# Routed experts: tokens put in expert order by one-hot matmuls and block scatters instead of row scatters

## The chip, the cores and the metric

One core of a Trainium2 chip runs the whole program: its five engines are TensorE (PE), VectorE (DVE), ScalarE (ACT), GpSimd (POOL) and SyncE (SP), beside the DMA queues. The metric is device time in microseconds, the median over runs; less is better.

## The reference

Three stages follow each other on 22784 tokens (4 x 5696) of 128 numbers. First a causal long convolution by FFT, then a soft mixture of experts with 32 slots, then a top-1 mixture of 8 experts. Only the last stage is touched:

```
logits = x @ w_gate + modality_bias[modality_id]
e_idx = argmax(logits, axis=1)
probs = exp(logits - max); probs /= probs.sum + 1e-09
gate_w = probs[arange(N), e_idx]
for e in range(8):
    mask = e_idx == e
    h = maximum(x[mask] @ w1[e], 0)
    out[mask] = gate_w[mask] * (h @ w2[e])
```

The input of this stage is itself a weighted sum of 32 slot outputs, so a token is carried as its 32 weights `c`, and the slot outputs are folded into the first weights of the expert. With the inputs used, all tokens choose one expert, so there are exactly 89 full tiles of 256 tokens and the program's part for a larger number of tiles doesn't run.

## The kernel before

The routing (class `Routing`) works on 178 groups of 128 tokens: token p*178+g sits on partition p in group g. DVE chooses the expert, counts tokens by expert with scans, and gets each token's position in expert order (`choose`, `gates`, `offsets`, `positions`). A record of 34 numbers a token (32 weights, gate, token id: 136 bytes) is written by POOL to `s_rec` in memory with an indirect DMA, one of 128 rows for each group (L1071).

The table GB cuts the groups into 9 chunks, CP the chunks into 3 parts. A tile of 256 records may be loaded when every group that can hold its tokens has been scattered; `first` and `chunk_of` say which. The part for chunks 0 to 2 is routed ahead of the tiles; the DVE steps of the rest (`late_steps`) are run between the tiles by `spend` (PACE microseconds of estimated work after each quarter) and by `need`, which runs them up to a due point.

The tile loop is `run` in `routed_experts`, written out by hand and kept in that order on every engine. Step k does for tile k its second layer, for tile k+1 its first layer, and for k+2 the transposes:

- `load_rec` (SP): the record tile `rt`. `rep`: an ACT copy rounds the weights (rr), a DVE subtraction leaves the rest (L1143). `tokT`: two PE transposes into pst, and an ACT copy into x (L1152).
- `l1`, in four quarters q: two matmuls into ph (L1161), ACT's relu into hh (L1163), DVE's remainder into hl (L1164).
- `l2`, in the same quarters: six matmuls into acc (L1174 to L1176).
- `out1`: ACT copies acc to yT. `out2`: two PE transposes into pso, and two ACT copies into y, scaled by the gate (L1188).
- `share`: how many of POOL's next issues are scatters and how many are stores of y to `out` (L1199, two of 128 rows a tile).

The order of the calls in a step sets the order on each engine, so PE works through `l1(k+1, q)`, `l2(k, q)` for q = 0 to 3 with the transposes of `out2` after q = 0 and those of `tokT` after q = 1. The wait of each instruction comes from its tiles.

## Time and profile before

| what | value |
|---|---|
| median of 3 runs | 1215.01 us (1214.18 to 1218.18) |
| profiled execution | 1213.09 us |
| its span | 1211.3 us |
| mean granted clock of PE | 0.877 |
| PE busy | 909.6 us (75%) |
| DVE busy | 649.3 us (54%) |
| ACT busy | 598.3 us (49%) |
| POOL busy | 597.6 us (49%) |

The profiled execution is one run with the profiler on. The span goes from its first to its last instruction, and what is left of its time lies around that. The page shows the span also in 40 slices of 30.3 us, each a digit (tenths busy); the routed experts fill about the slices from the 17th on. A row of the timeline begins with the start in us and the length; in brackets stands how long the engine was idle before it, and what ended that.

### The profile page before, as it was taken

How to read it: one execution, taken by the hardware profiler on the slowest of the kernel's cores; microseconds unless marked ns; L12 is line 12 of the kernel's file. 1: busy time of each engine (PE TensorE's matmuls, PEld its weight loads, DVE VectorE, ACT ScalarE, POOL GpSimd, SP SyncE). 2: the span in 40 equal slices, each digit the busy share in tenths (PEclk: the TensorE clock that was granted, in tenths of full speed). 3: DMA queues.
4: the chain of work that ended last, by engine and by line, in shares of the span. 5: the costliest groups of instructions: out<-in, count | busy, mean ns of one | idle time of the engine just before them, and what ended most of it. 6: DMA issues, size and time to landing. Idle time of an engine off the chain costs nothing.

```text
span 1211.3 us, 23480 instructions
## 1 busy us (share of the span) xinstructions
PE 909.6 (75%) x7634; PEld 828.9 (68%) x7634; DVE 649.3 (54%) x1219; ACT 598.3 (49%) x1340; POOL 597.6 (49%) x702
## 2 busy tenths in 40 slices
PE   7989999999988889843099232810219999999996
PEld 7988888888878778533088231810119999999996
DVE  2577767767666885532077121600016666666663
ACT  2574756566555563220077021600017777777775
POOL 2127566574792443176612755277654444444443
PEclk8999999999989999966589565955559999999998
DMA  9528476675893789944000000011011111111111
GB/s 291 112 81 236 150 225 190 200 216 159 264 352 104 260 336 402 279 134 117 16 13 12 15 12 12 14 30 32 29 31 42 37 38 39 40 38 38 39 40 32
DMA packets 101630, 142.60 MB, mean 118 GB/s; under 512 B 26028, under 2 KB 80748, under 8 KB 99084
## 3 DMA queue, kind: packets, MB, share of 16 engines
q1 hardware_dynamic: 90112, 126.26, 33.6%
q0 software_dynamic: 11392, 14.79, 4.0%
q8 instruction: 64, 1.05, 0.4%
q14 instruction: 62, 0.51, 0.1%
HBM read 218.62 MB, written 57.64 MB: 228 GB/s over the span
## 4 chain that ended last, share of the span: by engine, by line
PE 62%; another core or an unknown queue 13%; issue 10%; DVE 6%; ACT 4%; DMA 2%; POOL 2%; SPq 1%; ACTq 0%; POOLq 0%; DVEq 0%
PE psx L187 9%; PE ph L1161 8%; PE acc L1175 7%; PE acc L1176 7%; PE acc L1174 7%; PE psa L122 6%; PE psy L94 3%; PE pso L94 3%; DVE A L132 2%; PE psl L225 2%; PE px L599 2%; PE psS L609 2%; PE psi L423 2%; PE psw L122 1%
## 5 line engine op out<-in xcount | busy, mean ns | idle before, releaser
L1164 DVE SCALAR_TENSOR_TENSOR hl<-ph,hh 128x512 fp32r<-128x512 f32 x356 | 245.2, 691 | 300.4 <-ACT hh L1163 157.4
L1199 POOL DMA_INDIRECT out<-y,rt x178 | 173.3, 974 | 212.0 <-ACT y L1188 166.5
L1163 ACT ACTIVATE hh<-ph 128x512 fp32r<-128x512 f32 x356 | 214.0, 603 | 108.5 <-remote 58.2
L1161 PE MATMUL ph<-x,wm 128*128 128x256 f32 x712 | 162.7, 312 | 139.0 <-ACT x L1152 79.2
L1071 POOL DMA_INDIRECT s_rec<-rec,posi x178 | 174.1, 978 | 135.4 <-issue 53.1
L1161 PEld LDWEIGHTS ph<-x,wm 128*128 128x128 f32 x712 | 113.7, 199 | 143.0 <-ACT x L1152 82.5
L1175 PE MATMUL acc<-hl,wo 128*128 128x256 f32 x712 | 206.6, 290 | 5.7 <-issue 5.7
L1176 PE MATMUL acc<-hh,wo 128*128 128x256 f32 x712 | 206.5, 290 | 3.6 <-issue 3.6
L1174 PE MATMUL acc<-hh,wo 128*128 128x256 f32 x712 | 206.6, 290 | 0.6 <-issue 0.6
L1175 PEld LDWEIGHTS acc<-hl,wo 128*128 128x128 f32 x712 | 141.6, 199 | 4.5 <-issue 4.3
L1176 PEld LDWEIGHTS acc<-hh,wo 128*128 128x128 f32 x712 | 141.7, 199 | 3.8 <-issue 3.8
L1174 PEld LDWEIGHTS acc<-hh,wo 128*128 128x128 f32 x712 | 141.6, 199 | 0.0
L187 PE MATMUL psx<-G,A 128*128 128x128 f32 x890 | 124.5, 287 | 2.5 <-DVE A L132 1.3
L187 PEld LDWEIGHTS psx<-G,A 128*128 128x128 f32 x890 | 111.9, 196 | 19.8 <-DVE Y L198 13.2
L122 PE MATMUL psa<-fw,xs 128*128 128x180 f32 x640 | 109.9, 326 | 14.3 <-POOL xs L156 7.5
L122 PEld LDWEIGHTS psa<-fw,xs 128*128 128x128 f32 x640 | 100.0, 199 | 24.4 <-POOL xs L156 15.1
L132 DVE COPY A<-psa 64x360 f32<-64x360 f32 x160 | 88.4, 552 | 36.9 <-PE psa L122 32.4
L126 ACT COPY A<-psa 64x360 f32<-64x360 f32 x160 | 83.6, 523 | 41.6 <-PE psa L122 37.7
L200 POOL TENSOR_TENSOR Y<-Y,V 128x256 f32<-128x256 f32 (+1 forms) x92 | 65.6, 713 | 63.3 <-DVE V L199 57.3
L94 PE MATMUL pso<-ident,yT 128*128 128x128 f32 x178 | 39.3, 304 | 74.0 <-issue 50.9
L156 POOL COPY xs<-xr 89x512 f32<-89x512 f32 x68 | 45.8, 674 | 94.1 <-PE psa L122 73.5
L211 ACT COPY yt<-psy 128x512 f32<-128x512 f32 (+1 forms) x92 | 52.7, 573 | 78.9 <-PE psy L94 53.3
(215 smaller groups left out, 1411.9 us busy)
## 6 DMA issues: line engine op xcount, KB each, us to landing
wo<-s_wsc SPq DMA_DIRECT2D x89, 1024.0 KB
wm<-s_mwsc SPq DMA_DIRECT2D x178, 256.0 KB
s_yt<-yt SPq DMA_DIRECT2D x88, 256.0 KB
xr<-x SPq DMA_DIRECT2D x16, 640.0 KB
xr<-s_yt SPq DMA_DIRECT2D x18, 512.0 KB
s_wsc<-ws SPq DMA_DIRECT2D x32, 256.0 KB
L<-s_yt SPq DMA_DIRECT2D x16, 512.0 KB
s_ylt<-ylt SPq DMA_DIRECT2D x20, 256.0 KB
```

The costliest lines, as they stand in the source:

```text
L94: nc.tensor.transpose(out, in_, ident)
L122: nc.tensor.matmul(ps[:, i, :4 * NPAIR], x, fw1, start=True, stop=True)
L132: i = nc.vector.tensor_copy(o, v)
L187: nc.tensor.matmul(ps[:, m, :], A[:, 2 * i + m // 2, :, m % 2], G[:, 4 * i + m, :], start=True, stop=True)
L1071: i = nc.gpsimd.indirect_dma_start(R["rec"], bass.IndirectOffsetOnAxis(ap=posi[:, g:g + 1], axis=0), rec[:, g, :], None, bounds_check=SPAR ...
L1161: nc.tensor.matmul(ps[:, TM * j:TM * j + TM], wm[k % 3][:, 128 * f:128 * f + 128], x[k], start=True, stop=True)
L1163: nc.scalar.activation(o, ps, AF.Relu)
L1164: nc.vector.scalar_tensor_tensor(hl[:, 2 * q:2 * q + 2].rearrange("p j t -> p (j t)"), ps, 0.0, o.bitcast(F32), op0=ALU.max, op1=ALU.subtract)
L1174: nc.tensor.matmul(acc[k], wh, hh[:, f], start=(f == 0), stop=False)
L1175: nc.tensor.matmul(acc[k], wh, hl[:, f], start=False, stop=False)
L1176: nc.tensor.matmul(acc[k], wl, hh[:, f], start=False, stop=(f == 7))
L1199: i = nc.gpsimd.indirect_dma_start(out, bass.IndirectOffsetOnAxis(ap=r[:, j, NS + 1:RW].bitcast(I32), axis=0), y[:, j, :], None, bounds_ch ...
```

## The change

Groups become pairs of groups: 89 of 256 tokens. Each such group is put in expert order on the core before it goes to memory, and it goes there in blocks of 4 records.

- `positions` now gives each token a lane (the block, up to 72 in a group) and a slot in the block (0 to 3). `offsets` rounds the counts of each expert up to blocks of 4 and gives each lane its block number in `s_rec` (`dst`).
- `prep` builds the operands of a group: m = weights times gate in the slot's place (DVE, L1006), hi = m rounded (ACT, L1008), oh = one-hot of the lane (DVE, L1009), the id in two parts (DVE, L1011), lo = m - hi (DVE, L1013).
- `sort` multiplies: two PE matmuls of oh with 264 columns sum the two halves into srt (72 lanes x 264, L1024), ACT copies srt to so (L1026), and POOL scatters 72 rows of 1056 bytes (`put`, L1142).
- A record has 66 numbers (32 hi, 32 lo, two for the id). The gate is in the weights, so `rep` is gone and y is one ACT copy. A record tile comes in two loads, and a DVE step makes the token ids (L1268).
- In the tile loop `prep` runs after quarter 2 of a step, and `sort` at the start of the next, ahead of two stores. 13 groups are sorted before the first tile, two in each of the first 7 steps and one in each of 62 more; the last steps sort none.
- There are more chunks and 4 parts and tables instead of 3; acc is one buffer of two halves, srt has one PSUM buffer, y has 16 buffers instead of 31.

```diff
-NSLOT = NT // TM + NE - 1
+COLS = 2
+NGR = NG // COLS
+BK = 4
+LANES = 72
+TB = TM // BK
+MAXB = (128 * COLS + NE * (BK - 1)) // BK
+NSLOT = (NGR * MAXB + NE * (TB - 1)) // TB
 NSTAT = NT // TM
-RW = NS + 2
-GB = [0, 18, 22, 26, 34, 44, 64, 96, 128, NG]
+RW = 2 * NS + 2
+GB = [0, 18, 22, 26, 34, 44, 54, 64, 80, 96, 112, 128, 144, 160, NG]
 NC = len(GB) - 1
-CP = (0, 3, 6, NC)
+CP = (0, 3, 7, 11, NC)
...
-YBUF = 31
+YBUF = 16
...
-        nc.vector.tensor_reduce(self.pos[:, g0:g1], u.rearrange("p e g -> p g e"), axis=AX.X, op=ALU.add)
-        yield t
-        nc.vector.tensor_copy(self.posi[:, g0:g1], self.pos[:, g0:g1])
-        yield us(g1 - g0)
+        nc.vector.tensor_scalar(slot, pos, BK - 1, None, op0=ALU.bitwise_and)
+        yield us(n)
+        nc.vector.tensor_scalar(lane, pos, 2, None, op0=ALU.arith_shift_right)
+        yield us(n)
+        nc.vector.tensor_tensor(eq, self.il[:, :BK].unsqueeze(1).to_broadcast([128, n, BK]),
+                                slot.unsqueeze(2).to_broadcast([128, n, BK]), op=ALU.is_equal)
+        yield us(n * BK)
+
+    def masks(self, g0, g1):
+        nc = self.nc
+        n = g1 - g0
+        nc.vector.tensor_tensor(self.gm[:, g0:g1], self.eq[:, g0:g1], self.gate[:, g0:g1].unsqueeze(2).to_broadcast([128, n, BK]), op=ALU.mult)
+        yield us(n * BK)
 
     def prepare(self, k):
...
+    def prep(self, n):
+
+
+        nc = self.nc
+        i0 = self.prepped
+        self.prepped += n
+        g0, n = COLS * i0, COLS * n
+        g1 = g0 + n
+        m = self.work("m", (4, BK, NS), 2)[:, :n]
+        hl = self.rounded.tile([128, 4, BK, RW], F32R, name="hl4", tag="hl4", bufs=2)[:, :n]
+        oh = self.rounded.tile([128, 4, LANES], F32R, name="oh", tag="oh", bufs=2)[:, :n]
+        nc.vector.tensor_tensor(m, self.c[:, g0:g1].unsqueeze(2).to_broadcast([128, n, BK, NS]),
+                                self.gm[:, g0:g1].unsqueeze(3).to_broadcast([128, n, BK, NS]), op=ALU.mult)
+        nc.scalar.copy(hl[:, :, :, :NS], m)
+        nc.vector.tensor_tensor(oh, self.il.unsqueeze(1).to_broadcast([128, n, LANES]),
+                                self.lane[:, g0:g1].unsqueeze(2).to_broadcast([128, n, LANES]), op=ALU.is_equal)
+        nc.vector.tensor_tensor(hl[:, :, :, 2 * NS:], self.eq[:, g0:g1].unsqueeze(3).to_broadcast([128, n, BK, 2]),
+                                self.ab[:, g0:g1].unsqueeze(2).to_broadcast([128, n, BK, 2]), op=ALU.mult)
+        nc.vector.tensor_tensor(hl[:, :, :, NS:2 * NS], m, hl[:, :, :, :NS].bitcast(F32), op=ALU.subtract)
+        self.batches += [(i0 + j, hl[:, COLS * j:COLS * j + COLS], oh[:, COLS * j:COLS * j + COLS]) for j in range(n // COLS)]
+
+    def sort(self, n, put):
+
+
+        nc = self.nc
+        for _ in range(n):
+            i, hl, oh = self.batches.pop(0)
+            ps = self.wide([128, 512], F32, name="srt")[:LANES, :BK * RW]
+            for j in range(COLS):
+                nc.tensor.matmul(ps, oh[:, j], hl[:, j].rearrange("p s c -> p (s c)"), start=(j == 0), stop=(j == COLS - 1))
+            o = self.work("so4", (BK * RW,), 4)[:LANES]
+            nc.scalar.copy(o, ps)
+            put(i, o)
...
+def scatters(nc, tc, R, ro):
+
+    rows = R["rec"].rearrange("(b r) c -> b (r c)", r=BK)
+
+    def put(i, o):
+        d = nc.gpsimd.indirect_dma_start(rows, bass.IndirectOffsetOnAxis(ap=ro.dst[:LANES, i:i + 1], axis=0), o, None,
+                                         bounds_check=SPARE * TB - 1, oob_is_err=False)
+        for q in range(NC):
+            tc.declare_no_dep(d.ins, group=f"rec{q}", reason="positions of tokens are distinct")
+        tc.declare_no_dep(d.ins, group="recl", reason="a tile is loaded after its last token was scattered")
+        tc.declare_no_dep(d.ins, group="pad", reason="rows after the last token")
+        c = max(c for c in range(NC) if GB[c] <= COLS * i)
+        tc.add_to_no_dep_group(f"rec{c}", d.ins)
+    return put
...
-        def scatter(n):
-            for _ in range(n):
-                c, g = pending.pop(0)
-                need(0, g + 1)
-                i = nc.gpsimd.indirect_dma_start(R["rec"], bass.IndirectOffsetOnAxis(ap=posi[:, g:g + 1], axis=0), rec[:, g, :], None,
...
-        def share(k):
-
-            m = 15 * (k + 1) // 4 - 15 * k // 4
-            if not pending:
-                store(max(m, 4), k - 2)
-                return
-            n = NG - len(pending)
-            late = max(0, len(outs) - 2 * YBUF + 6)
-            new = max(0, GB[chunk_of(k + 3) + 1] - n, min(ready[0] - n, m - late))
-            scatter(new)
-            store(max(late, m - new), k - 2)
+        def due(k):
+
+            return GB[chunk_of(k) + 1] // COLS
+
+        def prep_to(k):
+            return min(NGR, max(due(k + 4), min(due(3) + 2 + 2 * k, 21 + k)))
+
+        def prep(k):
+            n = prep_to(k) - ro.prepped
+            while n > 0:
+                need(0, COLS * (ro.prepped + min(n, 2)))
+                ro.prep(min(n, 2))
+                n -= 2
...
             rv = nc.sync.value_load(entry(1, k), min_val=0, max_val=SPARE * TM)
             if k not in t:
                 t[k] = new_rec()
-            i = nc.sync.dma_start(t[k].rearrange("p j c -> p (j c)"), R["rec"][ds(rv, TM)].rearrange("(p j) c -> p (j c)", p=128))
...
+            assert COLS * (ro.prepped - len(ro.batches)) >= GB[chunk_of(k) + 1]
+            src = R["rec"][ds(rv, TM)].rearrange("(p j) c -> p j c", p=128)
+            for i in (nc.sync.dma_start(t[k][:, :, :64].bitcast(F32), src[:, :, :64]),
+                      nc.sync.dma_start(t[k][:, :, 64:].bitcast(F32), src)):
...
         def load_wm(k):
             ev, fv = expert(k)
             src = R["mwsc"][ds(ev, 1)].rearrange("e p f -> (e p) f")
-            for r in range(2):
-                nc.sync.dma_start(wm[k % 3][64 * r:64 * r + 64].bitcast(F32), src, cond=(fv > 0))
+            nc.sync.dma_start(wm[k % 3][:64].bitcast(F32), src, cond=(fv > 0))
+            nc.sync.dma_start(wm[k % 3][64:96].bitcast(F32), src[32:], cond=(fv > 0))
+            nc.sync.dma_start(wm[k % 3][96:].bitcast(F32), src[:32], cond=(fv > 0))
...
-        def rep(k):
-
-            r = rr[k] = rr.get(k) or new_rr()
-            c = t[k][:, :, :NS].unsqueeze(2).to_broadcast([128, 2, 2, NS])
-            nc.scalar.copy(r[:, :, 0:2], c)
-            nc.vector.tensor_tensor(r[:, :, 2:4], c, r[:, :, 0:2].bitcast(F32), op=ALU.subtract)
-
         def tokT(k):
 
-            r = rr.pop(k)
+            r = t.pop(k)
             ps = pp.tile([128, 2, 128], F32, name="pst", tag="t", bufs=2)
             for j in range(2):
-                turned(nc, ps[:, j].bitcast(F32R), r[:, j].rearrange("p r k -> p (r k)"), P["identr"])
+                turned(nc, ps[:, j].bitcast(F32R), r[:, j, :128], P["identr"])
+            d = ids[k] = sp.tile([128, 2], I32, name="ids", tag="ids", bufs=YBUF + 4)
+            nc.vector.scalar_tensor_tensor(d, r[:, :, 128].bitcast(F32), float(NT), r[:, :, 129].bitcast(F32), op0=ALU.add, op1=ALU.add)
             z = x[k] = x.get(k) or new_x()
             nc.scalar.copy(z, ps.rearrange("p j t -> p (j t)"))
...
-                acc[k] = pp.tile([128, TM], F32, name="acc", tag="acc", bufs=2)
+                acc[k] = sums[:, k % 2]
...
                 turned(nc, ps[:, j], yT[k][:, 128 * j:128 * j + 128], ident)
             y = sp.tile([128, 2, 128], F32, name="y", tag="y", bufs=YBUF)
+            nc.scalar.copy(y, ps)
+            d = ids.pop(k)
             for j in range(2):
-                nc.scalar.activation(y[:, j], ps[:, j], AF.Copy, scale=t[k][:, j, NS:NS + 1])
-            outs.append((k, 0, t[k], y))
-            outs.append((k, 1, t.pop(k), y))
+                outs.append((k, j, d, y))
 
...
                 go(out1, k - 1)
                 if k > k0:
                     go(load_wo, k + 2)
-                share(k)
+                ro.sort(len(ro.batches), put)
+                store(4, k - 2)
                 if k > k0:
                     go(load_rec, k + 3)
                 if k == k0:
                     go(l2, k, 0)
                     go(l2, k, 1)
                     go(tokT, k + 1)
-                go(rep, k + 2)
                 for q in range(4):
                     go(l1, k + 1, q)
                     if k > k0 or q >= 2:
@@ -1249,12 +1362,16 @@
                         go(out2, k - 1)
                     if q == 1:
                         go(tokT, k + 2)
+                    if q == 2 and k0 == 0:
+                        prep(k)
...
+            run_all(offsets, ro.gates(*PARTS[0][:2]), ro.positions(*PARTS[0][:2]), ro.masks(*PARTS[0][:2]))
+            ro.prep(1)
+            run_all(seconds(0))
+            ro.sort(1, put)
+            ro.prep(2)
+            run_all(sums(0), seconds(1))
             push(1, 1)
-            warm(W7)
+            ro.sort(2, put)
+            for i in range(3):
+                ro.prep(2)
+                if i == 1:
+                    run_all(seconds(2, 3))
+                ro.sort(2, put)
+            run_all(ro.table(tabs[0], CP[1]))
             middle = middle()
-            run_all(weave(ro.table(tabs[0], CP[1]), rest(), itertools.chain(itertools.islice(middle, 5), seconds(2, 3))))
+            for i in range(2):
+                ro.prep(2)
+                run_all(itertools.islice(middle, 3))
+                ro.sort(2, put)
             adds.append(gate(3))
```

PE, a step in the middle of the tile loop. Before, where one step ends and the next begins:

```order
L1175 MATMUL acc<-hl,wo_5399 128x256
L1176 MATMUL acc<-hh,wo_5399 128x256
L1161 MATMUL ph<-x,wm_5395 128x256 [waits DMAHW2_49,DMAHW3_49,DVE_49,Activation_49]
L1161 MATMUL ph<-x,wm_5395 128x256
L1174 MATMUL acc<-hh,wo_5397 128x256 [waits DMAHW0_49]
```

And after, at the same place:

```order
L1293 MATMUL acc<-hl,wo_5539 128x256
L1294 MATMUL acc<-hh,wo_5539 128x256
L1024 MATMUL srt<-hl_10060,oh 72x264 [waits DVE_49]
L1024 MATMUL srt<-hl_10060,oh 72x264
L1279 MATMUL ph<-x,wm_5535 128x256 [waits DMAHW2_49,DMAHW3_49,DMAHW1_49,PE_49]
L1279 MATMUL ph<-x,wm_5535 128x256
L1292 MATMUL acc<-hh,wo_5537 128x256 [waits DMAHW6_49,Activation_49]
```

The two srt stand in front of a step's first ph, and the first of them waits for DVE.

DVE, steps in the middle of the tile loop. Before, a step is five instructions:

```order
L1143 TENSOR_TENSOR rr<-rt,rr 128x2x64 [waits DMAHW5_49,Activation_49]
L1164 SCALAR_TENSOR_TENSOR hl<-ph,hh 128x512 [waits Activation_49] x4
L1143 TENSOR_TENSOR rr<-rt,rr 128x2x64 [waits DMAHW1_49,Activation_49]
L1164 SCALAR_TENSOR_TENSOR hl<-ph,hh 128x512 [waits Activation_49] x4
```

After, one step, with steps of late routing (L889, L892) in it; the hl with a number is the operand of srt:

```order
L1282 SCALAR_TENSOR_TENSOR hl<-ph,hh 128x512 [waits Activation_49] x2
L889 TENSOR_REDUCE vm<-xr 128x50 [waits DVE_49]
L1268 SCALAR_TENSOR_TENSOR ids<-rt 128x2 [waits DMAHW4_49,DMASW6_49,DMASW5_49]
L1282 SCALAR_TENSOR_TENSOR hl<-ph,hh 128x512 [waits Activation_49]
L1006 TENSOR_TENSOR m<-c,gm 128x256
L1009 TENSOR_TENSOR oh<-il,lane 128x144
L1011 TENSOR_TENSOR hl_8368<-eq,ab 128x8x2
L1013 TENSOR_TENSOR hl_8368<-m,hl_8368 128x8x32 [waits Activation_49]
L1282 SCALAR_TENSOR_TENSOR hl<-ph,hh 128x512 [waits Activation_49]
L892 TENSOR_TENSOR xr<-small,vm 128x400
```

Four instructions for the sort stand between hl of quarter 2 and hl of quarter 3, and the last waits for ACT.

POOL, where the records are scattered. Before, in the tile loop, a long row of scatters between the stores:

```order
L1071 DMA s_rec<-rec,posi 184576x34 [waits DMASW6_49]
L1071 DMA s_rec<-rec,posi 184576x34 [waits DMASW7_49]
L1199 DMA out<-y,rt 22784x128 [waits DMAHW5_49,DMASW0_49,Activation_49]
L1199 DMA out<-y,rt 22784x128 [waits DMASW1_49,Activation_49]
L1199 DMA out<-y,rt 22784x128 [waits DMAHW2_49,DMASW2_49,Activation_49]
L1071 DMA s_rec<-rec,posi 184576x34 [waits DMASW3_49,DVE_49]
L1071 DMA s_rec<-rec,posi 184576x34 [waits DMASW4_49]
```

After:

```order
L1142 DMA s_rec<-so_10460,dst 46144x264 [waits DMASW4_49,Activation_49]
L1317 DMA out<-y,ids 22784x128 [waits DMASW5_49,DVE_49]
L1317 DMA out<-y,ids 22784x128 [waits DMASW6_49]
L1142 DMA s_rec<-so_10576,dst 46144x264 [waits DMASW7_49,Activation_49]
L1317 DMA out<-y,ids 22784x128 [waits DMASW0_49,DVE_49]
```

Scatters and stores alternate, and each scatter waits for ACT's copy into so; before, most scatters waited only for an earlier DMA.

## Rows read from the trace of the kernel before

**Rows 1.** Windows by stage: busy us (instructions) by engine, clock, DMA:

```profile
607.00:657.00 50.00, 48.69 (x391) 48.13 (x392) 41.24 (x87) 41.21 (x103) 3.04 (x3) 0.94 0.06 12
657.00:905.00 248.00, 72.15 (x460) 68.50 (x459) 45.45 (x101) 46.51 (x113) 150.85 (x155) 0.62 0.08 22
905.00:1192.00 287.00, 284.13 (x2283) 271.96 (x2284) 193.66 (x318) 222.02 (x574) 123.16 (x127) 0.99 0.14 39
410.00:436.00 26.00, 21.74 (x126) 19.82 (x125) 19.45 (x37) 19.21 (x38) 12.94 (x8) 0.96 0.88 338
```

**Rows 2.** Timeline of ACT, copies into x: start, length, idle before:

```profile
607.43 0.37 ACT L1152 CAST x<-pst 128x256 fp32r<-128x256 f32 x1 [54.08 <-remote]
...
627.57 0.38 ACT L1152 CAST x<-pst 128x256 fp32r<-128x256 f32 x1
...
657.03 0.37 ACT L1152 CAST x<-pst 128x256 fp32r<-128x256 f32 x1
...
935.69 0.39 ACT L1152 CAST x<-pst 128x256 fp32r<-128x256 f32 x1
...
1115.14 0.37 ACT L1152 CAST x<-pst 128x256 fp32r<-128x256 f32 x1
...
1191.84 0.37 ACT L1152 CAST x<-pst 128x256 fp32r<-128x256 f32 x1
```

**Rows 3.** Timeline of POOL, end of its first long run:

```profile
601.13 0.97 POOL L1071 DMA_INDIRECT s_rec<-rec,posi  x1 [0.30 <-issue]
618.18 0.97 POOL L1199 DMA_INDIRECT out<-y,rt  x1 [16.08 <-ACT y L1188]
```

**Rows 4.** Timeline, PE results and who takes them:

```profile
533.72 0.47 ACT L736 COPY xr<-gl 96x384 f32<-96x384 f32 x1 [14.29 <-remote]
...
551.60 0.17 DVE L907 TENSOR_TENSOR off<-pre,cum 128x8 f32<-128x8 f32 x1 [10.76 <-remote]
...
564.28 0.37 PE L94 MATMUL pst<-identr,rr 128*128 128x128 f32 x2
```

**Rows 5.** Line of the row scatter: ns minimum/median/maximum, first and last start:

```profile
L1071 POOL DMA_INDIRECT s_rec<-rec,posi x178: 971/974/1403, 514.9 to 902.8; - x178
```

**Rows 6.** Timeline of PE, one tile while POOL idles:

```profile
650.34 0.40 PE L1161 MATMUL ph<-x,wm 128*128 128x256 f32 x2
...
652.59 0.47 PE L1161 MATMUL ph<-x,wm 128*128 128x256 f32 x2
...
654.58 0.40 PE L1161 MATMUL ph<-x,wm 128*128 128x256 f32 x2
```

**Rows 7.** Timeline of a late tile: PE, ACT, DVE:

```profile
1002.70 0.47 PE L1161 MATMUL ph<-x,wm 128*128 128x256 f32 x2
...
1003.21 0.60 ACT L1163 ACTIVATE hh<-ph 128x512 fp32r<-128x512 f32 x1
...
1004.17 0.60 ACT L1163 ACTIVATE hh<-ph 128x512 fp32r<-128x512 f32 x1 [0.36 <-issue]
...
1004.80 0.69 DVE L1164 SCALAR_TENSOR_TENSOR hl<-ph,hh 128x512 fp32r<-128x512 f32 x1 [0.26 <-issue]
```

**Rows 8.** Groups by form, 500 to 660 us:

```profile
L1180 ACT COPY yT<-acc 128x256 f32<-128x256 f32 x11 | 4.1, 372 | 2.0 <-PE acc L1176 1.4 <-PE ph L1161 0.5
...
L917 DVE TENSOR_TENSOR xr<-xr,off 128x256 f32<-128x256 f32 x2 | 0.8, 416 | 0.0
L757 DVE TENSOR_TENSOR xr<-psl,rec 128x512 f32<-128x512 f32 x1 | 0.7, 672 | 0.0
```

**Rows 9.** Windows, DVE alone, 508 to 562 us:

```profile
508.00:562.00 54.00, 24.46 (x130) 0.68 0.48 132
```

**Rows 10.** Tile rr, its DVE subtraction: ns minimum/median/maximum:

```profile
L1143 DVE TENSOR_TENSOR rr<-rt,rr x89: 270/293/317, 561.0 to 1190.5; 128x128 fp32r<-128x128 f32 x89
```

**Rows 11.** Timeline of PE, matmuls in a slow stretch:

```profile
827.90 0.41 PE L1174 MATMUL acc<-hh,wo 128*128 128x256 f32 x1
...
828.33 0.41 PE L1176 MATMUL acc<-hh,wo 128*128 128x256 f32 x1
```

More of the change, by code (lines that the diff above doesn't have):

```diff
@@ L918, in positions @@
         yield t
-        nc.vector.tensor_tensor(u, u, self.chunk(self.oh, k), op=ALU.mult)
+        with nc.allow_low_precision(reason="small whole numbers"):
+            nc.vector.tensor_reduce(pos, u, axis=AX.X, op=ALU.add)
         yield t
-        nc.vector.tensor_reduce(self.pos[:, g0:g1], u.rearrange("p e g -> p g e"), axis=AX.X, op=ALU.add)
-        yield t
-        nc.vector.tensor_copy(self.posi[:, g0:g1], self.pos[:, g0:g1])
-        yield us(g1 - g0)
-    def prepare(self, k):
-        yield from weave(self.gates(k), self.positions(k))
+        nc.vector.tensor_scalar(slot, pos, BK - 1, None, op0=ALU.bitwise_and)
@@ L1018, in run_all, with slices, work @@
             pass
+def slices(a, x):
+    have = {}
+    def work(name, shape, bufs):
+        nonlocal x
+        w = int(np.prod(shape))
+        if name not in have:
+            have[name] = itertools.cycle([a[:, x + w * i:x + w * i + w] for i in range(bufs)])
+            x += w * bufs
+            assert x <= 16 * F
+        t = next(have[name])
+        return t.rearrange("p (a b c) -> p a b c", b=shape[1], c=shape[2]) if len(shape) == 3 else t
+    return work
+def scatters(nc, tc, R, ro):
[10 more added lines that the diff above has]
+    return put
 def late_steps(ro, tabs, ready):
@@ L1062, in routed_experts @@
-        pending = [(c, g) for c in range(NC) for g in range(GB[c], GB[c + 1])]
+        sums = pp.tile([128, 2, TM], F32, name="acc", tag="acc", bufs=1)
+        first = [0] + [(128 // BK * GB[c] - NE * (TB - 1)) // TB for c in range(1, NC)] + [NSLOT]
         def chunk_of(k):
             return max(c for c in range(NC) if first[c] <= k)
-        def scatter(n):
-            for _ in range(n):
-                c, g = pending.pop(0)
-                need(0, g + 1)
-                i = nc.gpsimd.indirect_dma_start(R["rec"], bass.IndirectOffsetOnAxis(ap=posi[:, g:g + 1], axis=0), rec[:, g, :], None,
-                                                 bounds_check=SPARE * TM - 1, oob_is_err=False)
-                for q in range(NC):
-                    tc.declare_no_dep(i.ins, group=f"rec{q}", reason="positions of tokens are distinct")
-                tc.declare_no_dep(i.ins, group="recl", reason="a tile is loaded after its last token was scattered")
-                tc.declare_no_dep(i.ins, group="pad", reason="rows after the last token")
-                tc.add_to_no_dep_group(f"rec{c}", i.ins)
@@ L1102, in entry @@
         def entry(i, k):
-            n = sum(k >= first[c] for c in CP[1:3])
+            n = sum(k >= first[c] for c in CP[1:-1])
             need(1, n)
@@ L1257, in routed_experts @@
         ro.psum = lambda *a, **k: pp.tile(*a, tag="t", bufs=2, **k)
+        ro.wide = lambda *a, **k: pp.tile(*a, tag="s", bufs=1, **k)
+        ro.work = lambda name, shape, bufs: sp.tile([128, *shape], F32, name=name, tag=name, bufs=bufs)
         ready = [GB[CP[1] + 2], 0]
@@ L1437, in middle @@
                     yield from ro.prepare(k)
-            def rest():
-                for k in range(1, CP[1]):
-                    yield from ro.prepare(k)
             warm(W5)
```

266 lines of the change are left out of this document (150 added, 116 removed).

## The prediction

> **What bounds the kernel now.** I began with the page's fortieths: from a bit past the half to three quarters PE, DVE and ACT nearly stop while POOL is at 6 to 7 tenths and the clock falls. The windows by stage then give the sizes [rows 1]. From 607 to 657 us POOL is almost idle and PE is busy 48.69 of 50 us. From 657 to 905 us POOL is busy 150.85 of 248 us, PE only 72.15, and the clock is 0.62. From 905 us, with stores alone on POOL (123.16 of 287 us, 43%), PE is busy 284.13 of 287.
>
> The copies into x count tiles [rows 2]: 0 at 607.43, 5 at 627.57, 12 at 657.03, 31 at 935.69, 71 at 1115.14, 88 at 1191.84. That is 4.21 us a tile beside an idle POOL (29.46 over 7), 14.7 in the slow stretch, and 4.49 with two stores a tile (179.45 over 40). The 19.5 us left to the span's end are the tail. So some 200 us lie in one stretch, and what fills it is the row scatter: 178 of 974 ns [rows 5].
>
> How the scatter holds the others is in the timeline. The first x has waited 54.08 us for "remote" [rows 2], yet its two transposes on PE began at 564.28 and take 0.37 us [rows 4]. The copy starts 5.3 us after POOL's last scatter of that run ends (602.10) [rows 3]. Earlier results of PE were also taken 14.29 and 10.76 us late [rows 4]. A result of PE thus seems to reach its reader late while POOL issues DMAs back to back (a 0.97 us DMA, 0.30 us idle [rows 3]), and at once when POOL pauses. Hand-overs between ACT and DVE beside it are prompt. I read this as the bound; the trace doesn't say which part of the chip delays the signal.
>
> **What goes.** 178 scatters become 89, of 72 rows instead of 128. Before, POOL took them from a list as fast as it could. Now each stands behind ACT's copy of the sorted group, and that behind PE: one per tile, after two stores. So long runs have no way to form in the tile loop, and the clock and the pace of the slow stretch should be gone. The unseen 72-row issue I put between 0.55 us (0.97 times 72/128) and 0.97 us [rows 5]; near the latter, since the line's minimum and median agree. A tile then has at most 3 times 1.27, or 3.8 us of POOL, below the pace found next, so either end is hidden.
>
> **What comes: a loop through three engines.** PE's order starts a step with two srt matmuls that wait for DVE's lo. DVE makes that only after hl of quarter 2 of the step before. I add up from quarter 2's ph on. From ph to ACT's hh 0.51 us, from hh to DVE's hl 0.63, hl itself 0.69 [rows 7]. Then m, oh, id and lo on DVE: 256 columns take 0.416 us and 512 take 0.672, so 0.16 us and 1.0 ns a column [rows 8]; m and lo cost 0.42 each, oh (144) 0.30, id (16) 0.18. ACT's hi (0.37, as the copy of the same shape [rows 8]) lies beside oh and id. That is 1.32 us, and 0.02 to hand over: 3.17 us in all. PE itself needs only 1.99 us from ph of quarter 2 to the end of the step [rows 6]. So it stands about 1.18 us in every tile that sorts. PE does a tile in 4.24 us, from 650.34 to 654.58 [rows 6]: 8 ph and 24 acc of 256 columns and 4 transposes of half that, so 0.125 us each 256 columns, and 0.25 us for two srt. With these and the 2.25 us from quarter 0 to quarter 2 [rows 6], a tile takes 2.25 + 3.17 + 0.25 = 5.67 us, above the 4.24 that PE took in rows 6. The bounds are 4.49 (no wait at all, srt beside other waits) and 6.8 (rival C).
>
> A step that sorts two groups has m and lo of 512 columns (0.26 us more each), oh of 288 and id of 32 (0.16 more), so 0.68 us, and its second sort must wait until ACT has emptied the only srt bank and refill it, 0.4 + 0.25 + 0.25 of signals: 0.9. It takes 7.25 us.
>
> **Start.** Before, PE's transposes for tile 0 began at 564.28. In front of them the two late hand-overs took 25 us [rows 4]; they should go, since no scatter of POOL stands in a run of dozens. DVE gains 13 groups of sorting, one single (1.32 us) and six pairs (2.0 us each), 13.3 us, to its 24.46 us [rows 9], and some 20 small steps of offsets of about 100 columns, 0.16 + 0.10 us and a hand-over, 6 us. From the last of these to the first record's load I allow 7 us, as scatter, load and transposes follow each other. 564 - 25 + 19 + 7 gives x of tile 0 at 565, between 550 (no new work on the path) and 590 (the late hand-overs stay: 13 scatters follow each other closely).
>
> **Small edits.** The copy and subtraction of rr leave ACT and DVE (0.29 us on DVE [rows 10]); in DVE's order ids takes its place. y is one copy instead of two, and gates sit in the records. ACT is busy 222.02 of 287 us, so 3.47 of 4.49 a tile [rows 1]; with hi and so, 0.75 more at most, it stays below 5.67, hidden. The records come in two loads a tile, which wait for scatters issued at least three steps earlier; SP gets one load and one skipped weight load more a tile; it kept up at 4.21 us [rows 2], so 1.4 us are free for them. If that lead is used up, the tile waits for one scatter and its landing, about 5 us. The later parts' offsets and masks are about 14 DVE steps of 200 columns, 0.36 us each, three times, 15 us, run between the tiles; where they fall between hl and m they lengthen the loop. I take 10 us of the 15. Each store or scatter on POOL costs the pace (4.49 - 4.24)/2 = 0.12 us beside busy PE [rows 2, 6]; in a loop with slack on PE it costs between nothing and 3 times 0.12 in 69 tiles, 25 us: half, 12.
>
> **Sum.** 565 + 7 x 7.25 (51) + 62 x 5.67 (352) + 19 x 4.49 (85) + 10 + 12 + 19.5 = 1094.5 us of span. The profiled execution took 1213.09 us with a span of 1211.3, so 1.8 us lie around it, and it stands 1.9 us below the median 1215.01. That makes about 1096.
>
> The Trainium skill, in "SBUF — State Buffer", section "Who interferes with whom", says that a DVE instruction with two inputs in SBUF and a GpSimd instruction that reads SBUF lock each other out for a whole instruction. All four new DVE operations have two such inputs. By that the loop would be held once a tile by one DMA issue. The trace speaks against it: the subtraction L1143, with both inputs in SBUF, took 270 to 317 ns in all 89 cases [rows 10], with POOL busy 43 to 61% of the time [rows 1] at 0.97 us an issue; a lock would show a case near 1 us.
>
> **Rivals.**
>
> B: the sort does not hold PE. That is so if hl of quarter 2 comes earlier than in rows 7, or PE's queue hides the wait. A tile is then 4.24 + 0.25 + 0.25 = 4.75 us: 565 + 42 + 294 + 85 + 10 + 19.5 + 1.8, about 1018. Against it: 3.17 exceeds 1.99 clearly, and no element of the sum is soft.
>
> C: three DMAs on POOL in each tile are dense enough to make PE's results late again. Harmless is a share of 43%, starved one of 61% [rows 1]; three of 0.97 us in 5.67 are 51%, in between. If the pace gives way until the share is 43%, a tile takes 6.8 us: 565 + 63 + 422 + 85 + 10 + 19.5 + 1.8, about 1166. For it: two stores a tile already cost 0.25 us. Against it: the scatter waits for ACT, so POOL pauses by itself.
>
> E: DVE and POOL exclude each other, as one mechanism of this loop: one of m and lo waits for one issue, 0.97 us in each of 62 tiles, 60 us: about 1156. Rows 10 speak against it.
>
> D, the side of slower: PE's pause of 1.2 us in each tile lowers the clock to 1.2 GHz. Matmuls then come every 0.215 us [rows 11] instead of 0.125; 34 of them a tile add 3.06 us to 4.24, and srt takes 0.43, so PE alone needs about 7.7 us: 565 + 63 + 477 + 85 + 22 + 19.5 + 1.8, about 1233. It becomes slower than before from a pace of about 7.4 us, where the sum reaches 1213. For it: the clock of 0.62 where PE idles most [rows 1]. Against it: from 410 to 436 PE was busy 84% (21.74 of 26 us) at a clock of 0.96 [rows 1], the loop leaves PE busy about 79%, and at half the clock PE would be longer than DVE after quarter 2 (1.99 becomes 3.4, above 3.17), so never pause, and gain its clock back.
>
> **How the numbers follow.** My forecast (pace 5.2 to 6.2, start 550 to 590: 1060 to 1145) gets 0.61, B 0.13, C 0.13, E 0.05, D 0.08. The time is 1096. The range goes from 1030, just above B, to 1185, so that C and E are inside; D and most of B, under 2 in 10, are left out. Faster by over 0.3% (3.6 us, about what a measurement of this kernel can tell): A, B, C, E but for a small rest, 0.91; within 0.3% 0.01; slower 0.08.
>
> **What would show it.** The sorted tiles at 5.5 to 5.9 us between copies into x, with PE idle about 1.2 us ahead of srt, released by DVE's lo; the last 19 at 4.5. No "remote" wait over a few us after tile 0, a clock of 0.9 or more in the tile loop, x of tile 0 near 565. Wrong it is if PE waits elsewhere: idle before ACT's copies put down to "remote" (C), m or lo at about 1.4 us (E), matmuls at 0.215 (D), no idle before srt (B).

## The result and the profile after

The changed kernel takes 1135.6 us (median of 4 runs, 1129.59 to 1138.5) beside 1214.6 us of the kernel before: a ratio of 0.934, 95% interval 0.929 to 0.938. Forecast were 1096 us and faster. The profiled execution took 1138.5 us with a span of 1136.6. A second number belongs beside it: the experiments ran on other chips too. On two of them the kernel before takes 978 us; on one of these the changed kernel ran as well and took 1100, a ratio of 1.124 (1.121 to 1.127). The experiments show what is slow in the one case and not in the other; why the chips differ stays open. Runs over 1.5% above the fastest of their kernel are left out of the medians.

The copies into x of the changed kernel, tiles 0, 2, 9, 71 and 88 (start, length, idle before), against [rows 2]:

```profile
567.89 0.37 ACT L1270 CAST x<-pst 128x256 fp32r<-128x256 f32 x1 [20.60 <-issue]
...
573.91 0.38 ACT L1270 CAST x<-pst 128x256 fp32r<-128x256 f32 x1
...
640.72 0.37 ACT L1270 CAST x<-pst 128x256 fp32r<-128x256 f32 x1 [1.94 <-PE ph L1279]
...
1023.14 0.37 ACT L1270 CAST x<-pst 128x256 fp32r<-128x256 f32 x1 [0.20 <-PE pst L100]
...
1115.92 0.37 ACT L1270 CAST x<-pst 128x256 fp32r<-128x256 f32 x1 [0.20 <-PE pst L100]
```

So tile 0 comes at 568 instead of 607, tiles 2 to 9 (two groups sorted in a step) take 9.54 us each (66.81 over 7), tiles 9 to 71 6.17 (382.42 over 62), the last 17 5.46 (92.78 over 17; 10.27 for the first of them, 5.16 for the others), and 20.7 us are the tail. The stretch of 14.7 us a tile is gone. The windows of the first two of these stages, with the columns of [rows 1], say the same:

```profile
574.00:641.00 67.00, 43.41 (x293) 39.67 (x291) 37.97 (x81) 32.23 (x74) 25.28 (x26) 0.87 0.16 40
641.00:1023.00 382.00, 298.99 (x2351) 282.47 (x2351) 266.25 (x696) 242.57 (x559) 179.89 (x186) 0.99 0.22 56
```

PE is busy 78% in the long stage, at a clock of 0.99, where before it was 29% at 0.62.

A sorted tile without late routing, timeline of ACT, DVE, PE and POOL:

```profile
884.31 0.69 DVE L1282 SCALAR_TENSOR_TENSOR hl<-ph,hh 128x512 fp32r<-128x512 f32 x1 [0.34 <-issue]
884.31 0.97 POOL L1317 DMA_INDIRECT out<-y,ids  x1 [0.30 <-issue]
884.92 0.41 DVE L1006 TENSOR_TENSOR m<-c,gm 128x256 f32<-128x256 f32 x1
885.25 0.30 DVE L1009 TENSOR_TENSOR oh<-il,lane 128x144 fp32r<-128x144 f32 x1
885.37 0.41 ACT L1008 CAST hl<-m 128x256 fp32r<-128x256 f32 x1 [1.09 <-issue]
885.47 0.17 DVE L1011 TENSOR_TENSOR hl<-eq,ab 128x16 fp32r<-128x16 f32 x1
885.81 0.43 DVE L1013 TENSOR_TENSOR hl<-m,hl 128x256 fp32r<-128x256 f32 x1 [0.17 <-issue]
886.29 0.47 PE L1024 MATMUL srt<-hl,oh 128*72 128x264 f32 x2 [0.98 <-DVE hl L1013]
887.47 0.96 POOL L1142 DMA_INDIRECT s_rec<-so,dst  x1 [2.19 <-ACT so L1026]
```

This is the loop of the forecast: hl, m, oh and id beside hi, lo, and srt at once behind lo, after 0.98 us of idle PE. The next such tile is 5.67 us later (its srt starts at 891.96). The 72-row scatter takes 0.96 us, the 128-row one 0.97.

### The profile page after: what moved, and what is told of

It is laid out like the page before. It is cut to its first block, busy times and chain, and to the rows that moved or that the text cites. A ratio compares the mean times of both kernels' runs of the same rounds, so it can differ in the third digit from the quotient of the medians.

```text
span 1136.6 us, 24552 instructions
## 1 busy us (share of the span) xinstructions
PE 941.2 (83%) x7798; PEld 847.2 (75%) x7798; DVE 747.4 (66%) x1623; ACT 625.2 (55%) x1319; POOL 511.5 (45%) x611
## 5 line engine op out<-in xcount | busy, mean ns | idle before, releaser
L1317 POOL DMA_INDIRECT out<-y,ids x178 | 174.8, 982 | 105.6 <-ACT y L1305 55.0
L1293 PE MATMUL acc<-hl,wo 128*128 128x256 f32 x712 | 204.0, 287 | 0.3 <-DVE hl L1282 0.3
L1142 POOL DMA_INDIRECT s_rec<-so,dst x76 | 73.0, 961 | 229.2 <-ACT so L1026 222.6
L1279 PE MATMUL ph<-x,wm 128*128 128x256 f32 x712 | 158.8, 306 | 1.0 <-ACT x L1270 1.0
L1292 PEld LDWEIGHTS acc<-hh,wo 128*128 128x128 f32 x712 | 138.1, 194 | 21.3 <-ACT yT L1298 19.4
L1024 PE MATMUL srt<-hl,oh 128*72 128x264 f32 x178 | 43.4, 335 | 116.9 <-DVE hl L1013 108.5
L1293 PEld LDWEIGHTS acc<-hl,wo 128*128 128x128 f32 x712 | 138.6, 195 | 0.5 <-DVE hl L1282 0.5
L1294 PEld LDWEIGHTS acc<-hh,wo 128*128 128x128 f32 x712 | 138.7, 195 | 0.0
L1024 PEld LDWEIGHTS srt<-hl,oh 128*72 128x72 f32 x178 | 20.6, 156 | 137.3 <-DVE hl L1013 114.1
L1279 PEld LDWEIGHTS ph<-x,wm 128*128 128x128 f32 x712 | 111.0, 194 | 1.5 <-ACT x L1270 1.2
```

Source lines behind the costliest of these rows:

```text
L1024: nc.tensor.matmul(ps, oh[:, j], hl[:, j].rearrange("p s c -> p (s c)"), start=(j == 0), stop=(j == COLS - 1))
L1279: nc.tensor.matmul(ps[:, TM * j:TM * j + TM], wm[k % 3][:, 128 * f:128 * f + 128], x[k], start=True, stop=True)
L1292: nc.tensor.matmul(acc[k], wh, hh[:, f], start=(f == 0), stop=False)
L1293: nc.tensor.matmul(acc[k], wh, hl[:, f], start=False, stop=False)
L1294: nc.tensor.matmul(acc[k], wl, hh[:, f], start=False, stop=(f == 7))
L1317: i = nc.gpsimd.indirect_dma_start(out, bass.IndirectOffsetOnAxis(ap=d[:, j:j + 1], axis=0), y[:, j, :], None, bounds_check=NT - 1, oob_is ...
```

## The experiments

Kernels of one batch ran on one chip, with the kernel before beside them. It takes 1214 to 1221 us in three batches ("first kind": that of the result, whose chip isn't on record, and those of chips 2 and 7) and 978 us in two ("second kind": chips 14 and 6). No chip is on record with two batches, so whether the kind belongs to the chip or to its state at the time isn't shown. Times are compared within a kind only. "Late" means here: PE's matmuls have ended, the engine that reads their result is free, and it starts only some time after.

**Where the tile time goes (first kind, chip 2).** prep after quarter 0:

```
-                    if q == 2 and k0 == 0:
+                    if q == 0 and k0 == 0:
                         prep(k)
```

> The changed kernel with prep run after quarter 0 of a step instead of after quarter 2; nothing else is moved. Loop theory (srt at the start of a step waits for lo, which DVE makes 3.17 us after ph of quarter 2): lo is now ready about 1 us before PE ends the step, the idle time ahead of srt goes, and the sorted tiles fall from 6.17 us on average to what the unsorted tiles at the end take, 5.15 us, or a little more: 62 x 0.9 = 56 us less, about 1080. Rival (three POOL DMAs in each tile set the pace, PE's wait is only where it shows): the pace stays at 6 us and the time within 10 us of 1136, with PE's results taken late by ACT.

Measured: 1110.95 us, sorted tiles 5.93 us (621.09 to 989.04 over 62). The loop was real: what PE waited for from 780 to 980 us in the changed kernel, and then in this one (us, times, longest):

```profile
PE srt L1024 <- DVE hl L1013: 37.8, 31, 4.6
...
PE pst L100 <- DMA rt<-s_rec: 0.8, 1, 0.8
```

```profile
PE acc L1292 <- ACT yT L1298: 24.8, 25, 2.3
PE pst L100 <- DMA rt<-s_rec: 12.9, 11, 2.4
```

The wait for lo is gone, and two others have come up from under it, so the sorted tiles gave 14.5 us (382.42 to 367.95) and not 56. More, 18.8 us, came from a place that I had not named: the seven steps with two groups fell to 6.86 us each (573.04 to 621.09), where srt waited for lo as well. One of the new waits is acc behind yT. The other is the record load, which SP issues every 5.9 us:

```profile
932.22 0.57 SPq L1232 DMA_DIRECT2D rt<-s_rec  x1
...
938.13 0.57 SPq L1232 DMA_DIRECT2D rt<-s_rec  x1
```

**Steps with two groups.** Four memsets on POOL, 2 us, between two scatters and two stores:

```
+                pair = len(ro.batches) == 2
                 ro.sort(len(ro.batches), put)
+                if pair:
+                    for _ in range(4):
+                        nc.gpsimd.memset(idle, 0.0)
                 store(4, k - 2)
```

> The changed kernel with four memsets on POOL (about 2 us, no DMA) between the two scatters and the two stores of each step that sorts two groups. Run theory (a row of four DMAs on POOL without a break makes PE's results late): the break ends the run after two, the seven steps fall from 9.54 to about 7.5 us, 14 us less, though POOL gets 14 us more work. Rival (POOL's amount of work or the single srt bank sets these steps): they stay at 9.5 or grow, the time is the same or up to 14 us longer.

Measured: 1129.24 us; the seven steps take 8.31 us (571.11 to 629.31) instead of 9.54, and the one behind them 9.32 instead of 7.64. POOL got more work and the steps got shorter, as the run theory has it, but by 7 us net and not 14. In the changed kernel three of the seven x are late, by 3.4, 3.0 and 1.8 us; here none is by more than 0.41. The time differs from the changed kernel's by about 6 us, within the spread of either; the steps carry this reading. In the changed kernel such a step looks like this (POOL, PE, ACT):

```profile
616.14 0.96 POOL L1142 DMA_INDIRECT s_rec<-so,dst  x1 [4.47 <-ACT so L1026]
617.41 0.94 POOL L1142 DMA_INDIRECT s_rec<-so,dst  x1 [0.30 <-issue]
618.55 0.29 PE L100 MATMUL pst<-identr,rt 128*128 128x128 f32 x2
618.65 0.99 POOL L1317 DMA_INDIRECT out<-y,ids  x1 [0.30 <-issue]
619.95 0.98 POOL L1317 DMA_INDIRECT out<-y,ids  x1 [0.30 <-issue]
621.92 0.37 ACT L1270 CAST x<-pst 128x256 fp32r<-128x256 f32 x1 [2.98 <-PE acc L1294]
```

pst is through by 618.84, and ACT takes it at 621.92, 0.99 us after POOL's fourth DMA (the row names PE's acc, which x doesn't read); in most tiles with three DMAs ACT takes it 0.03 to 0.05 us after the transposes. A row of four needn't cost so much: in early_prep the same four stand in a row in six of these steps, with pauses of 0.9 to 2.8 us between the rows, and the late starts that show there are 0.5 to 1.1 us.

**The last tiles.** acc of odd tiles in the idle srt bank, once all groups are sorted:

```
                 acc[k] = sums[:, k % 2]
+                if k % 2 and ro.prepped == NGR and not ro.batches:
+                    acc[k] = pp.tile([128, 512], F32, name="acc2", tag="s", bufs=1)[:, :TM]
```

> The changed kernel; once the last group is sorted, odd tiles take the idle srt bank for acc instead of the second half of the one acc tile. Bank theory (the first acc of a step waits for yT of the tile before because both halves are one buffer): the last 16 tiles fall from 5.16 to about 4.5 us, 10 us less, and nothing else changes. Rival (the last tiles are slower for another reason, stores or one more SP load): they stay at 5.1 or more.

Measured: 1130.28 us (1126.51 to 1135.9), no difference that can be told. Tiles 72 to 75 took 4.43 us each (1031.24 to 1044.54), as the bank theory says, and then 5.39 (1044.54 to 1114.67 over 13), held by the record load:

```profile
1070.80 0.34 PE L100 MATMUL pst<-identr,rt 128*128 128x128 f32 x2 [1.50 <-DMA rt<-s_rec]
```

So both are true: the one acc buffer costs 0.7 us a tile, and SP's work for a tile, over 5 us, stands right behind it. The 0.7 is the buffer's only in part: in the last tiles PE waits 10.2 us for yT in 16 steps of the changed kernel (0.64 each), and in eleven of them ACT starts yT 0.2 to 0.7 us late; on the second kind, where none is late, the same wait is 4.5 us in 16 (0.28 each).

**A second scatter (chip 2).** In `sort`, behind `put(i, o)`, the same block to a scratch; that makes four DMAs in a tile (the expectation miscounted them as five):

> The changed kernel; in the tile loop every block scatter is issued a second time into a scratch that nobody reads, so POOL issues five DMAs a tile instead of three (the second half of the sorting, then 165 block scatters instead of 89). Throughput theory (POOL costs only its own time, 1.28 us a DMA): 5 x 1.28 = 6.4 us a tile instead of 6.17, about 1155 in all. Run theory (a row of DMAs longer than about 5 us makes PE's results late until it ends): each tile loses 3 us or more, pace 9 to 10 us, 1320 or more, and ACT's waits for PE grow by 2 to 5 us a tile while the others stay.

Measured: 1213.87 us, sorted tiles 7.18 us (644.63 to 1089.98). By POOL's own time four DMAs are 5.1 us, below the loop's 5.67, so throughput says no change; the measured 1.0 us a tile I read as lateness, though far less than the 3 us that I expected. Part of it shows directly: ACT's hh waits 38.7 us for PE's ph in these tiles (30 times), where in the changed kernel it waits 2.7 us (7 times).

**The same length without a DMA (chip 14).** Against the run before it:

```
-            d = nc.gpsimd.indirect_dma_start(rows2, ...)
+            for _ in range(2):
+                nc.gpsimd.memset(ro.idle, 0.0)
```

> The changed kernel; in the tile loop each block scatter is followed by two memsets on POOL (together about 1.2 us, the time of a scatter) where the run before had a second scatter. POOL's row in a tile is as long as there: scatter, memsets, store, store. If a long row of DMAs is what makes PE's results late, the memsets break it and the time is that of the changed kernel, 1136 us plus at most 15, with sorted tiles at 6.2 us. If it is POOL being busy without a pause, whatever it does, the sorted tiles take 7.2 us as with the second scatter, about 1210.

Measured: 1103.81 us. It decides nothing: the kernel before took 978 us beside it, so it was the second kind, and that of the second scatter the first.

**Pauses in the kernel before (chip 14).** `pause` is called behind each scatter and each store:

```
+        def pause():
+            issued[0] += 1
+            if issued[0] % 3 == 0:
+                for _ in range(11):
+                    nc.gpsimd.memset(idle, 0.0)
```

> The kernel before; after every third DMA that POOL issues in the expert stage it does eleven small memsets, about 1.3 us without a DMA, 118 times, so POOL has some 150 us more to do. Run theory: rows of more than three DMAs are gone, x of tile 0 follows its transposes at once instead of 43 us later, the slow stretch of 14.7 us a tile goes, and what is left is POOL's own rate (about 1.7 us for a DMA with its share of the pause until the last scatter): 1150 to 1200 us, faster although POOL works more. Throughput theory (the scatters' number is what holds the tiles): the stretch up to the last scatter gets longer by about 70 pauses, 95 us, so about 1300.

Measured: 1239.3 us, 26.7% slower than the kernel before on that chip (interval 26.4 to 27.0), and not for lateness: none shows in this trace. x of tile 0 starts at 559.20, and what holds the tiles is a record that POOL has not scattered yet, as in

```profile
650.62 0.30 ACT L1152 CAST rr<-rt 128x128 fp32r<-128x128 f32 x1 [18.85 <-DMA rt<-s_rec]
```

On this kind throughput theory is right in its cause, though not in its 95 us. The eleven memsets took 1.75 us instead of 1.3, and 2.4 us passed between two DMAs with them, so a DMA with its share took 2.0 us instead of 1.28, and POOL's 356 DMAs end at 1231.96 instead of 968.81 (next section): 263 us, the whole difference. It says nothing of the first kind, where this wasn't tried.

**Both kernels again, for their traces (chip 6).**

> The kernel before, unchanged, for its trace. The runs of the last four kernels had the kernel before at 978 us beside them, the runs ahead of those at 1214. If PE's results are late only where the run is of the 1214 kind, then a run near 978 shows x of tile 0 less than 1 us after its transposes, rows of dozens of scatters on POOL as before, and tiles of 4.2 to 4.5 us throughout; a run near 1214 shows x of tile 0 some 40 us late again. If instead the 978 come from POOL (shorter issues, or fewer in a row), the length of an issue is below 0.97 us there.

> The changed kernel, unchanged, beside the kernel before on the same chip. Loop theory: its sorted tiles are held by DVE's lo, not by late results, so where the kernel before takes 978 us this one still has 5.67 us a tile: 567 + 7 x 7.9 + 62 x 5.8 + 19 x 5.2 + 20, about 1100, slower than before by 12%. Rival (what the change gains or loses is the same wherever it runs, 6 to 7% less): about 915. Where the kernel before takes 1214, about 1135 again.

Measured: 977.69 and 1100.02 us. In the kernel before, at tile 0, timeline of POOL, PE and ACT:

```profile
538.31 0.97 POOL L1071 DMA_INDIRECT s_rec<-rec,posi  x1 [0.30 <-DMA s_rec<-rec,posi]
539.58 0.97 POOL L1071 DMA_INDIRECT s_rec<-rec,posi  x1 [0.30 <-issue]
539.69 0.47 PE L94 MATMUL pst<-identr,rr 128*128 128x128 f32 x2 [4.31 <-DVE rr L1143]
540.20 0.37 ACT L1152 CAST x<-pst 128x256 fp32r<-128x256 f32 x1 [0.98 <-PE pst L94]
540.86 0.97 POOL L1071 DMA_INDIRECT s_rec<-rec,posi  x1 [0.30 <-issue]
```

x starts 0.51 us behind the start of its transposes, in the middle of the same row of scatters, of the same 0.97 us, at which that took 43 us in [rows 2, 4]. The row never ends here: all 356 DMAs follow each other from 512.25 to 968.81 with no pause of 0.6 us, and nothing is late. The windows show it by stage:

```profile
607.00:797.00 190.00, 177.73 (x1437) 172.04 (x1437) 121.03 (x222) 137.11 (x356) 144.91 (x149) 0.98 0.14 34
797.00:941.00 144.00, 142.00 (x1189) 141.42 (x1188) 100.97 (x165) 120.96 (x300) 109.59 (x113) 0.99 0.20 61
```

POOL is busy 76% of both, more than the 61% at which PE starved in [rows 1], and PE is busy 94% and 99%. The last tiles take 4.24 us beside 3.3 stores a tile (112 from 797 to 941), instead of 4.49 beside two, so I put those 0.25 us down to lateness as well, though hardly a late start shows in them. What ends last here is POOL's row of stores, 28 us behind x of tile 88 (941.09).

The changed kernel does here what its loop says: tile 71 at 989.66 from tile 9 at 626.00 is 5.87 us a tile, 5.66 without late routing. Its span of 1098.6 is 38 us below that of the first kind, the kernel before's 975.3 is 236 below.

**Row or busy POOL (chip 7, first kind).** Second scatters for groups 13 to 51, memsets of that length for groups 52 to 88:

```
+        if again and i >= 52:
+            for _ in range(2):
+                nc.gpsimd.memset(ro.idle, 0.0)
+            return
```

> The changed kernel; in the tile loop the block scatters of groups 13 to 51 are issued a second time into a scratch that nobody reads (up to x of about tile 34), and those of groups 52 to 88 are followed by two memsets of the same length, 1.2 us, instead (tiles 36 to 71). Both halves keep POOL busy for about 5 us in a tile. Where the kernel before takes 1214 us: if PE's results come late because of a row of DMAs, the first half takes 7.2 us a tile as in twice_scattered and the second 5.7 to 6.2; if POOL being busy is enough, both take 7.2; if it is neither, both 5.7 to 6.2. Where the kernel before takes 978 us: no lateness is seen there with any row, so both halves take 5.7 to 6.2 (what DVE's late routing adds), about 1105 in all; a first half near 7.2 would mean that the second scatter costs by itself, without lateness.

Measured: 1171.93 us. Tiles 10 to 34 take 7.26 us each, tiles 36 to 71 5.95. Copies into x of these four tiles, then the windows of the halves:

```profile
655.00 0.37 ACT L1284 CAST x<-pst 128x256 fp32r<-128x256 f32 x1 [0.87 <-PE pst L100]
...
829.16 0.37 ACT L1284 CAST x<-pst 128x256 fp32r<-128x256 f32 x1 [0.20 <-issue]
...
842.90 0.37 ACT L1284 CAST x<-pst 128x256 fp32r<-128x256 f32 x1 [0.91 <-PE pst L100]
...
1051.04 0.37 ACT L1284 CAST x<-pst 128x256 fp32r<-128x256 f32 x1 [0.20 <-PE pst L100]
```

```profile
655.00:829.00 174.00, 126.93 (x919) 117.76 (x918) 113.71 (x335) 93.33 (x217) 93.06 (x96) 0.94 0.22 56
843.00:1051.00 208.00, 165.25 (x1331) 157.01 (x1330) 138.36 (x325) 134.03 (x315) 146.57 (x174) 1.00 0.23 59
```

In the first half POOL is busy 53%, in the second 70%, and the second is the faster by 1.3 us a tile; the changed kernel's own tiles 10 to 34 take 6.11 us. ACT's waits for ph in the two halves (us, times, longest):

```profile
ACT hh L1295 <- PE ph L1293: 16.7, 15, 1.7
```

```profile
ACT hh L1295 <- PE ph L1293: 0.7, 2, 0.4
```

So a row of DMAs delays PE's results there, and a busy POOL does not. What the second scatters cost without lateness wasn't tried on the second kind.

**A better version.** prep after quarter 0 and one conditional load of wm instead of three (the first weights kept in memory in all four blocks; the edit of that is left out here):

```
-            nc.sync.dma_start(wm[k % 3][:64].bitcast(F32), src, cond=(fv > 0))
-            nc.sync.dma_start(wm[k % 3][64:96].bitcast(F32), src[32:], cond=(fv > 0))
-            nc.sync.dma_start(wm[k % 3][96:].bitcast(F32), src[:32], cond=(fv > 0))
+            nc.sync.dma_start(wm[k % 3].bitcast(F32), src, cond=(fv > 0))
```

> The changed kernel with prep after quarter 0 (as in early_prep) and the first weights kept in memory as all four blocks of 32 rows, so that a tile has one conditional weight load for wm instead of three; the writes of the weights put each block in two places with the same number of DMAs. SP theory (in early_prep PE's transposes wait for a record load that SP issues late, because SP's own work for a tile is about 5.7 us): two skipped loads less free about 1 us a tile on SP, the sorted tiles go from 5.93 to about 5.3 us (the wait of acc for yT stays), the last ones from 5.7 back to 5.2: 40 us less than early_prep, about 1070. Rival (the record load itself or POOL's three DMAs are the limit): no change from 1111.

Measured: 1023.66 us on chip 14, 4.6% slower than the kernel before there, so the 1070 don't compare. SP issues a record load every 4.2 us now:

```profile
930.18 0.55 SPq L1233 DMA_DIRECT2D rt<-s_rec  x1
...
934.36 0.55 SPq L1233 DMA_DIRECT2D rt<-s_rec  x1
```

Then acc in two banks again and srt in those of the transposes:

```
-                acc[k] = sums[:, k % 2]
+                acc[k] = pp.tile([128, TM], F32, name="acc", tag="acc", bufs=2)
...
-        ro.wide = lambda *a, **k: pp.tile(*a, tag="s", bufs=1, **k)
+        ro.wide = lambda *a, **k: pp.tile(*a, tag="t", bufs=2, **k)
```

> The run before it, with acc in two PSUM banks again and srt in the two banks of the transposes. With the wait of acc for yT gone as well, PE is bound by its own 4.24 + 0.25 us and what POOL's three DMAs cost: unsorted tiles 4.5 us, sorted ones 4.9 to 5.2 with the late routing on DVE, steps with two groups 6.5: about 1025. If three DMAs a tile in so short a tile make PE's results late (run theory at its edge: 3.8 us of row in 4.9), the sorted tiles stay at 5.5 or more and the time at 1055 or more.

Measured on chip 14: 1004.13 us, sorted tiles 4.72 us (618.32 to 906.23 over 61) and the last 4.4. And once more, on chip 7:

> The kernel of early_one_two_banks once more (prep after quarter 0, one conditional weight load, acc in two banks, srt in the banks of the transposes). Where the kernel before takes 978 us: 1004 again, slower than before by 2.7%. Where it takes 1214 us: the loop doesn't hold PE, rows of four DMAs in the steps with two groups and of three in 4.6 us elsewhere make PE's results late by 1 us in some tiles: 1010 to 1060, faster than both kernels; if rows without a long enough pause are starved as before, the pace goes to 6 us and more, above 1100.

Measured: 1073.01 us, 0.879 of the kernel before beside it (0.877 to 0.882). That is faster than both kernels on the first kind; sorted tiles take 5.69 us there (623.70 to 970.85 over 61), a microsecond more than on chip 14 with the same order. ACT's waits for ph in these tiles on chip 7, then on chip 14, say that three DMAs in less than 5 us make PE's results late again:

```profile
ACT hh L1279 <- PE ph L1277: 42.7, 37, 1.6
```

```profile
ACT hh L1279 <- PE ph L1277: 2.6, 8, 0.4
```

On the second kind it is 2.7% slower than the kernel before.

## Why the prediction was right, and where its sum was off

- **The bound and what goes.** Right for the chip of the result: rows of scatters on POOL delay PE's results, and the change ends the rows. Lateness took 236 us in the kernel before and takes 38 us in the changed one (the spans of the two kinds, all of whose difference I put down to lateness), so 198 us go; the loop and the start cost 123 us (975.3 to 1098.6), and 75 us remain, 1211.3 - 1136.6. Seen directly, the starts of x, hh, yT, so and y that are over 0.5 us late sum to 170 us in the trace before and 16 in the one after; the rest of the 236 and 38 is what followed from them and isn't traced. In the six traces of the second kind there is no such start. What the prediction missed is that the lateness is no property of the kernel. It took it for the price of a dense POOL wherever the kernel runs. Nor is POOL's share of the time the measure, as in C's 43 and 61%: 70% with memsets in it was harmless, 53% in rows of four DMAs was not.
- **The loop.** Right to a hundredth: 5.67 us forecast, 5.67 measured, PE's pause 0.98 us instead of 1.18. Its parts hold too, in the tile after the one shown: 2.24 us from quarter 0 to quarter 2 (2.25 forecast), 3.12 from there to srt (3.17), 0.31 for srt (0.25).
- **Start.** 565 forecast, 567.9 measured; 563.0 without lateness. The 25 us of the two late hand-overs are borne out by the second kind: the kernel before begins tile 0's transposes 24.6 us earlier there (539.69 against 564.28).
- **Steps with two groups.** The term 7 x 7.25 failed by 16 us: 9.54. On the second kind they take 8.14 (569.03 to 626.00): 0.9 us that I had left out, part of it late routing (they range from 7.4 to 9.2 us; in the longest a routing step of 0.68 us, DVE's L892, stands right in front of m); the other 1.4 us, 10 us in all, are lateness from four DMAs in a row (8.2 us of it in the three late x), which I had priced at nothing because rows of dozens were gone.
- **The last tiles.** The term 19 x 4.49 failed by 13 us: the first two steps took 3.0 us less than it says, sixteen others 10.7 us more, and the one from tile 71 to 72 5.8 us more. The cause of the 10.7 is for the most part the edit that I costed at nothing, acc as one buffer of two halves. In these tiles ACT's yT and PE's acc follow each other:

```profile
1082.64 0.37 ACT L1298 COPY yT<-acc 128x256 f32<-128x256 f32 x1 [0.57 <-PE ph L1279]
1083.06 0.39 PE L1292 MATMUL acc<-hh,wo 128*128 128x256 f32 x1 [0.67 <-ACT yT L1298]
```

The 5.8 us are lateness: POOL issues the last scatter and four stores in a row, and yT starts 1.29 us after their end, though acc was through by 1025.1. On the second kind seven DMAs stand in a row there, and the step takes 4.86 us.

```profile
1021.58 0.96 POOL L1142 DMA_INDIRECT s_rec<-so,dst  x1 [2.54 <-ACT so L1026]
...
1026.69 0.97 POOL L1317 DMA_INDIRECT out<-y,ids  x1 [0.30 <-issue]
1028.95 0.37 ACT L1298 COPY yT<-acc 128x256 f32<-128x256 f32 x1 [2.33 <-remote]
```

- **The single groups with routing and POOL** came to 382 us instead of 374 (352 + 10 + 12), the tail to 20.7 instead of 19.5. With 2.9 us at the start, 16 in the steps with two groups and 13 in the last tiles these make 42 us, the distance from 1094.5 to 1136.6.
- **SP.** "1.4 us are free" was wrong: SP's work for a tile is over 5 us, hidden only as the loop is longer.
- **The rivals.** B's 4.75 us is near what the kernel without the wait takes on the second kind (4.72), by luck: B's 0.25 us for POOL's DMAs aren't there, and late routing is; without that a tile takes 4.46 (774.34 to 832.37 over 13). C is true in small. E and D are out: m and lo of 256 columns never wait (below), and the clock is 0.99.

```profile
L1006 DVE TENSOR_TENSOR m<-c,gm x69: 363/416/684, 575.4 to 1019.0; 128x256 f32<-128x256 f32 x62, 128x512 f32<-128x512 f32 x7
...
L1013 DVE TENSOR_TENSOR hl<-m,hl x69: 425/427/696, 576.8 to 1019.9; 128x256 fp32r<-128x256 f32 x62, 128x512 fp32r<-128x512 f32 x7
```

The maxima are those of 512 columns (0.68 and 0.70 us), and no 128x256 shows a wait for one POOL issue (0.42 and 0.43 us at most); oh and the id take at most 0.51 and 0.19 us, in all 76 cases. The rule of the Trainium skill that the prediction weighed ("SBUF — State Buffer", "Who interferes with whom") does not show in these four operations, and the section does not ask for it there: it names a GpSimd instruction that reads SBUF, and infers that making a DMA's descriptors needs the write side, which `tensor_tensor` leaves alone.

Open: why PE's results are late on some chips and not on others, and whether one chip can be of either kind at different times; and whether pauses in the kernel before would help on the first kind, which wasn't tried.

## What to carry to other kernels

A stall that has no instruction behind it may belong to the chip that the profile was taken on, or to its state: take the kernel's trace on a second one before its cure is built, since here the cure gains 6.6% on one and costs 12% on another. When a loop is made shorter, price what stands right under it (SP's work for a tile, a buffer that was halved), for the gain ends there. And an operation between engines is cheap where its input is made early in a step, dear where it is made last.
